# Decoding float64 weights: the rebiased bits in a PSUM buffer of the transposes, the three low bits from ScalarE

## The chip, the cores and the metric

The kernel runs on one core of a Trainium2 chip. The metric is the device time of one execution in microseconds (us). The core's engines each work through their own queue in order: TensorE (PE in the profile, its weight loads as PEld), VectorE (DVE), ScalarE (ACT), GpSimd (POOL); SyncE (SP) issues the loads. All but GpSimd reach PSUM, the memory that TensorE writes, which has eight banks of 128 x 512 fp32; all reach SBUF.

## The reference

Sliding-window attention with a linear position bias (8 batches, 8 heads, 576 positions, 64 per head), then a feed-forward block over its 4608 x 512 output. q, k and v arrive as float32, the weights `w_in` and `w_out` as float64, and the output is float32.

```
scores = q @ k.T / 8 - slope[h] * |i - j|        where 0 <= i - j < 128, else -1e9
attn   = softmax(scores)
x      = (attn @ v), heads side by side           # 4608 x 512
h      = x @ w_in                                 # w_in 512 x 2048
out    = (h * sigmoid(1.702 * h)) @ w_out         # w_out 2048 x 512
```

## The kernel before

The host hands over the weights as the raw 64-bit words of their float64 values, cut into 16 blocks of `w_in` and 16 of `w_out` (each 128 x 512 words). `fetch` (line 201) loads a block into SBUF with an SP transfer; `decode` (line 210) makes fp32 of it on the chip and then splits that into a rounded part and the rest, both in TensorE's fp32 format, so that a product can be summed from three matmuls.

A float64 is two 32-bit words. The upper one (`top`) holds the sign, the 11 bits of the exponent and the first 20 of the mantissa; the lower one (`low`) holds the rest, of which an fp32 needs the three uppermost. The steps of one block, by line:

- L218, ScalarE: `top`, read as an fp32, times 2 to the power of -112. This takes the difference of the two exponents' offsets off, and goes to `c`, a tile of 128 x 512 of the SBUF pool's tag "o" (three buffers, shared with `xb` of L410 and L411).
- L219, VectorE: `low` shifted right by 29, in place; its three uppermost bits are left.
- L220, VectorE: `c` shifted left by 3, or-ed with `low`.
- L221, VectorE: the sign bit of `top` or-ed into `c`. Now `c` is the fp32.
- L224, ScalarE: `c` rounded into the first half of `res`. L225, GpSimd: `c` less that, into the second half.

Attention runs in units of one to three blocks of rows. A function `tick` (line 510) does one step of a pipeline over the units: scores on TensorE (`s_ps`, L303 and L309), the bias and the row minimum on VectorE (L321), the exponent on ScalarE (L332), the division by the row sum (L340, L341, then L345 on GpSimd for the first 24 units, L347 on ScalarE or L349 on VectorE for others), the transposes on TensorE (`flip`, L364) into a PSUM tile `t_ps` of which there are two buffers, their way out (L375 on ScalarE, and for all but the first 24 units the rest on VectorE, L381), and the product with v (L393, L398). PSUM is full: two banks for `acc`, two for `h_ps`, one for `s_ps`, one for `x_ps`, two for `t_ps`.

The feed-forward block works on chunks of 256 rows (`Job`): for each of 16 blocks f, `up` (12 matmuls, L452, then L457 on ScalarE, L458 on VectorE, L461 on ScalarE, L462 on GpSimd) and `down` (6 matmuls, L471). `split_x` (L436, L438) prepares a chunk.

The main loop (from line 585) goes through the pairs of job and block in order. Ahead of each it decodes as many blocks as the weights' due times ask for (`owed`, line 588), and does as many ticks as the due times of attention's outputs ask for (`pace`). Blocks 0 of both weights are decoded in the loop before it. The first chunk uses only the first 8 blocks at first and gets the others after the second chunk, so that the last weights are due later. So the 32 decodings lie in the first part of the program, beside the attention of the first two batches and the first steps of the feed-forward block.

The kernel writes no waits: the framework (Tile) derives them from the tiles. It also sets the order of the instructions on each engine, by a simulated timeline made when the program is built (`schedule_with_timeline_sim=True`), in which an instruction that opens a tile waits until one of its tag's buffers is free. Only the SP transfers keep the program's order (`move`).

Of the kernel before, what the change touches and what calls it, by code (L numbers as in the profile page):

```python
# [8 lines left out]
F32 = mybir.dt.float32  # L9
F32R = mybir.dt.float32r  # L10
BF16 = mybir.dt.bfloat16
I32 = mybir.dt.int32
I64 = mybir.dt.int64
AF = mybir.ActivationFunctionType
ALU = mybir.AluOpType
PSUM = bass.MemoryType.PSUM
# [4 lines left out]
P = 128  # L21
# [135 lines left out]
def tile_kernel(ctx: ExitStack, tc: tile.TileContext, qT, kT, v, w_in, w_out, out):  # L157
    nc = tc.nc
# [5 lines left out]
    ffn = ctx.enter_context(tc.tile_pool(name="ffn", bufs=2))  # L164
    ps = ctx.enter_context(tc.tile_pool(name="ps", bufs=1, space=PSUM))

    def move(dst, src):

        tc.keep_in_program_order(nc.sync.dma_start(dst, src))
# [4 lines left out]
    bias = [const.tile([P, 2 * P], BF16, name=f"bias{h}") for h in range(H)]  # L174
# [26 lines left out]
    def fetch(src, name):  # L201
        st = const.tile([P, 512], I64, name="r" + name, tag=name)
        move(st, src)
        return st
# [5 lines left out]
    def decode(st, name):  # L210

        words = st.bitcast(I32).rearrange("p (m two) -> p m two", two=2)
        top, low = words[..., 1], words[..., 0]
        c = ffn.tile([P, 512], I32, name="wc", tag="o", bufs=3)

        nc.scalar.activation(c.bitcast(F32), top.bitcast(F32), AF.Copy, scale=2.0 ** -112)  # L218
        nc.vector.tensor_scalar(low, low, 29, None, ALU.logical_shift_right)  # L219
        nc.vector.scalar_tensor_tensor(c, c, 3, low, ALU.logical_shift_left, ALU.bitwise_or)  # L220
        nc.vector.scalar_tensor_tensor(c, top, -0x80000000, c, ALU.bitwise_and, ALU.bitwise_or)  # L221
        w = c.bitcast(F32)
        res = const.tile([P, 2, 512], F32R, name=name, tag=name)
        nc.scalar.copy(res[:, 0], w)  # L224
        nc.gpsimd.tensor_tensor(res[:, 1], w, res[:, 0].bitcast(F32), ALU.subtract)  # L225
        return res
# [101 lines left out]
    def exponents(u):  # L328
        u.sums = att.tile([P, 2], F32, name="sums", bufs=3)
        for e, b in enumerate(u.blocks):  # L330
            live = b.p[:b.rows, b.live:b.end]
            nc.scalar.activation(  # L332
                live, live, AF.Exp, bias=u.mins[:b.rows, e:e + 1], scale=-1.0,
                accum_out=u.sums[:b.rows, e:e + 1],
            )

    def normal(u, on_act):
# [4 lines left out]
        for e, b in enumerate(u.blocks):  # L342
# [3 lines left out]
            elif on_act:  # L346
                nc.scalar.activation(live, live, AF.Copy, scale=u.rec[:rows, e:e + 1])  # L347
            else:
# [92 lines left out]
    class Job:  # L441
# [6 lines left out]
        def up(self, f):  # L448
# [7 lines left out]
            g = ffn.tile([P, T], F32, name="g")  # L456
            nc.scalar.activation(g, h, AF.Tanh, scale=0.851)  # L457
            nc.vector.scalar_tensor_tensor(g, g, 1.0, h, ALU.add, ALU.mult)  # L458
# [97 lines left out]
    while ticks < due[0][0] + 3:  # L556
        tick()
        spin(SPINS)
        fetch_upto(ticks - FETCH_TICK)
        if ticks == DECODE_TICK:  # L560
            w1[0] = decode(w1[0], f"w1_0")
        if ticks == DECODE_TICK + 1:
            w2[0] = decode(w2[0], f"w2_0")
# [21 lines left out]
    for now, (j, f) in enumerate(flat):  # L585

        if halves < 2 * NF:
            owed += max(
                (2 * g + 2 - halves - owed) / max(need[g] - DECODE_AHEAD - now, 1)
                for g in range(halves // 2, NF))  # L590
            while owed >= 1 and halves < 2 * NF:
                owed -= 1
                g, ws = halves // 2, (w1, w2)[halves % 2]
                fetch_upto(g + 1 + FETCH_AHEAD)
                ws[g] = decode(ws[g], f"w{1 + halves % 2}_{g}")
                halves += 1
# [64 lines left out]
```

## Time and profile before

| | |
|---|---|
| time, median of 3 runs | 1099.26 us (1097.17 to 1099.34) |
| span of the profiled execution, first to last instruction | 1094.0 us |
| its own time | not recorded; the median is 5.3 us above the span |
| mean granted TensorE clock | 0.990 |

The profile's page first gives the busy time of each engine, then the span in 40 slices of 27 us with the busy share in tenths, then DMA, the chain of work that ended last, and the costliest groups of instructions: line, engine, operation, tiles written and read, shape, count, busy time, mean duration, and the idle time of the engine just before them with the instruction that ended it. A busy TensorE isn't one at its peak, since the ends of pipelined matmuls are modelled. Idle time of an engine that is not the bound costs nothing.

### The profile page before, as it was taken

How to read it: one execution, taken by the hardware profiler on the slowest of the kernel's cores; microseconds unless marked ns; L12 is line 12 of the kernel's file. 1: busy time of each engine (PE TensorE's matmuls, PEld its weight loads, DVE VectorE, ACT ScalarE, POOL GpSimd, SP SyncE). 2: the span in 40 equal slices, each digit the busy share in tenths (PEclk: the TensorE clock that was granted, in tenths of full speed). 3: DMA queues.
4: the chain of work that ended last, by engine and by line, in shares of the span. 5: the costliest groups of instructions: out<-in, count | busy, mean ns of one | idle time of the engine just before them, and what ended most of it. 6: DMA issues, size and time to landing. Idle time of an engine off the chain costs nothing.

```text
span 1094.0 us, 21796 instructions
## 1 busy us (share of the span) xinstructions
PE 1059.8 (97%) x7021; PEld 944.6 (86%) x7021; DVE 745.2 (68%) x2331; ACT 592.2 (54%) x1765; POOL 658.9 (60%) x931
## 2 busy tenths in 40 slices
PE   8888889999999999999999999999999999999998
PEld 5565668999998999999999998999999999998997
DVE  4999798778898687754575768676877677423131
ACT  4665565566675665543555556655565556322222
POOL 4998877567677666644565666665666666323232
PEclk9999889999999999999999999999999999999999
DMA  5965213232242222201222222221222212000000
GB/s 142 332 171 160 69 46 86 72 82 74 84 105 86 65 84 65 84 23 48 54 67 53 84 55 84 65 84 51 73 76 65 76 46 78 1 20 20 1 20 19
DMA packets 97265, 81.24 MB, mean 74 GB/s; under 512 B 50048, under 2 KB 88448, under 8 KB 97152
## 3 DMA queue, kind: packets, MB, share of 16 engines
q1 hardware_dynamic: 91968, 70.42, 23.4%
q10 hardware_dynamic: 5184, 9.44, 2.3%
q8 instruction: 55, 0.90, 0.4%
q14 instruction: 58, 0.48, 0.1%
HBM read 70.39 MB, written 9.44 MB: 73 GB/s over the span
## 4 chain that ended last, share of the span: by engine, by line
PE 82%; DVE 3%; issue 1%; POOL 0%; ACT 0%; DVEq 0%; POOLq 0%
PE h_ps L452 34%; PE acc L471 34%; PE x_ps L398 5%; PE s_ps L309 5%; PE t_ps L364 4%; DVE pb L349 0%; DVE xh L436 0%; DVE pb L321 0%; DVE K L294 0%; DVE rec L340 0%; DVE xf L429 0%; DVE wc L221 0%; DVE g L458 0%; DVE pl L381 0%; DVE o L487 0%
## 5 line engine op out<-in xcount | busy, mean ns | idle before, releaser
L452 PE MATMUL h_ps<-xh,w 128*128 128x256 f32 x2304 | 370.5, 285 | 8.8 <-DVE g L458 4.2
L462 POOL TENSOR_TENSOR gl<-g,gh 128x256 fp32r<-128x256 f32 x288 | 218.6, 759 | 262.2 <-ACT gh L461 198.2
L452 PEld LDWEIGHTS h_ps<-xh,w 128*128 128x128 f32 x2304 | 329.5, 189 | 41.2 <-DVE g L458 6.6
L471 PE MATMUL acc<-w,gh 128*128 128x512 f32 x1152 | 326.8, 401 | 1.1 <-DVE xf L479 1.1
L458 DVE SCALAR_TENSOR_TENSOR g<-g,h_ps 128x256 f32<-128x256 f32 x288 | 119.4, 415 | 181.3 <-ACT g L457 179.6
L457 ACT ACTIVATE g<-h_ps 128x256 f32<-128x256 f32 x288 | 109.8, 382 | 209.7 <-PE h_ps L452 192.4
L471 PEld LDWEIGHTS acc<-w,gh 128*128 128x128 f32 x1152 | 197.6, 189 | 28.7 <-issue 1.3
L452 PE MATMUL h_ps<-xl,w 128*128 128x256 f32 x1152 | 195.9, 281 | 0.0
L461 ACT CAST gh<-g 128x256 fp32r<-128x256 f32 x288 | 116.7, 405 | 145.9 <-DVE g L458 136.4
L471 PE MATMUL acc<-w,gl 128*128 128x512 f32 x576 | 189.0, 403 | 0.0
L332 ACT ACTIVATE pb<-pb,mins 128x256 f32<-128x256 f32 (+3 forms) x292 | 141.2, 484 | 64.9 <-DVE mins L321 61.7
L296 POOL TENSOR_TENSOR K<-rk,K 128x384 fp32r<-128x384 f32 (+1 forms) x140 | 127.3, 909 | 80.7 <-ACT Q L276 24.9
L452 PEld LDWEIGHTS h_ps<-xl,w 128*128 128x128 f32 x1152 | 164.2, 189 | 5.8 <-DVE xl L438 0.3
L321 DVE CUSTOM_DVE_ANT_0 pb<-s_ps,bias 128x256 f32<-128x256 f32 (+5 forms) x320 | 114.2, 376 | 14.7 <-PE s_ps L309 6.5
L349 DVE TENSOR_SCALAR pb<-pb,rec 128x256 f32<-128x256 f32 (+2 forms) x252 | 110.1, 473 | 3.5
L295 POOL TENSOR_TENSOR Q<-rq,Q 64x256 fp32r<-64x256 f32 (+1 forms) x140 | 98.0, 700 | 21.6 <-ACT Q L276 4.4
L364 PE MATMUL t_ps<-ident,pb 128*128 128x128 f32 (+1 forms) x548 | 100.8, 275 | 8.2 <-DVE pb L349 6.6
L471 PEld LDWEIGHTS acc<-w,gl 128*128 128x128 f32 x576 | 93.0, 190 | 8.0 <-issue 0.5
L340 DVE TENSOR_SCALAR rec<-sums 128x2 f32<-128x2 f32 (+2 forms) x164 | 55.1, 336 | 59.6 <-ACT pb L332 58.4
L309 PE MATMUL s_ps<-K,Q 128*128 128x256 f32 (+1 forms) x504 | 91.9, 290 | 2.6 <-POOL gl L462 1.4
L381 DVE TENSOR_TENSOR pl<-t_ps,ph 128x512 fp32r<-128x512 f32 (+2 forms) x140 | 84.0, 602 | 5.2 <-ACT ph L375 4.8
L294 DVE CAST K<-rk 128x384 fp32r<-128x384 f32 (+1 forms) x140 | 59.0, 422 | 41.0 <-PE s_ps L309 31.6
(56 smaller groups left out, 1305.7 us busy)
## 6 DMA issues: line engine op xcount, KB each, us to landing
rk<-kT SPq DMA_DIRECT2D x84, 192.0 KB, 2.7
rq<-qT SPq DMA_DIRECT2D x112, 128.0 KB, 2.6
out<-o ACTq DMA_DIRECT2D x36, 256.0 KB, 2.1
rw<-w_in SPq DMA_DIRECT2D x16, 512.0 KB, 5.9
rw<-w_out SPq DMA_DIRECT2D x16, 512.0 KB, 7.0
rk<-kT SPq DMA_DIRECT2D x56, 128.0 KB, 2.3
rv<-v SPq DMA_DIRECT2D x100, 64.0 KB, 2.0
rq<-qT SPq DMA_DIRECT2D x44, 64.0 KB, 2.4
```

What stands on the lines that cost most here:

```text
L296: nc.gpsimd.tensor_tensor(K2, rk, K1.bitcast(F32), ALU.subtract)
L309: nc.tensor.matmul(u.s[:b.rows, e, b.first:b.end], u.Q[:, b.q0 - u.q0:b.q0 - u.q0 + b.rows], k[:, ko:ko + b.end - b.first], start=(z == 0) ...
L321: nc.vector.tensor_tensor_reduce(b.p[ra:rb, cs:b.end], u.s[ra:rb, e, cs:b.end], bias[head][ra:rb, cs:b.end], -SCALE, BIG, ALU.add, ALU.min ...
L332: nc.scalar.activation(live, live, AF.Exp, bias=u.mins[:b.rows, e:e + 1], scale=-1.0, accum_out=u.sums[:b.rows, e:e + 1],)
L349: nc.vector.tensor_scalar(live, live, u.rec[:rows, e:e + 1], None, ALU.mult)
L364: nc.tensor.transpose(u.t[:c.n, w:w + b.rows], b.p[:b.rows, col:col + c.n], ident[:b.rows, :b.rows])
L452: nc.tensor.matmul(h, w1[f][:, z, k * P:(k + 1) * P], x[:, k], start=(n == 0), stop=(n == len(ops) - 1))
L457: nc.scalar.activation(g, h, AF.Tanh, scale=0.851)
L458: nc.vector.scalar_tensor_tensor(g, g, 1.0, h, ALU.add, ALU.mult)
L461: nc.scalar.copy(gh, g)
L462: nc.gpsimd.tensor_tensor(gl, g, gh.bitcast(F32), ALU.subtract)
L471: nc.tensor.matmul(acc, g[:, t * P:(t + 1) * P], w2[f][:, z], start=(f == self.f0 and n == 0), stop=(f == self.f1 - 1 and n == 2))
```

## The change

The rebiased bits (`c` before) get a PSUM tile of the transposes' tag `t_ps`, one of the same two buffers, and the fp32 result a tile of tag "o" of its own, from L221 on. The three low bits come from ScalarE instead of VectorE's shift: a copy reads `part`, the upper 16 bits of `low`, as an integer, multiplies it by 2 to the power of -13, subtracts not quite a half, and rounds to an integer, which is that word's upper three bits; it writes it over `low`. L220 and L221 do the same operations as before, L220 in place in PSUM, L221 from PSUM and SBUF into SBUF. L224 and L225 are the same.

```diff
+U16 = mybir.dt.uint16
...
         words = st.bitcast(I32).rearrange("p (m two) -> p m two", two=2)
         top, low = words[..., 1], words[..., 0]
-        c = ffn.tile([P, 512], I32, name="wc", tag="o", bufs=3)
-        nc.scalar.activation(c.bitcast(F32), top.bitcast(F32), AF.Copy, scale=2.0 ** -112)
-        nc.vector.tensor_scalar(low, low, 29, None, ALU.logical_shift_right)
-        nc.vector.scalar_tensor_tensor(c, c, 3, low, ALU.logical_shift_left, ALU.bitwise_or)
-        nc.vector.scalar_tensor_tensor(c, top, -0x80000000, c, ALU.bitwise_and, ALU.bitwise_or)
-        w = c.bitcast(F32)
+        part = st.bitcast(U16).rearrange("p (m four) -> p m four", four=4)[..., 1]
+        bits = ps.tile([P, 4 * P], F32, name="w_ps", tag="t_ps", bufs=2).bitcast(I32)
+        w = ffn.tile([P, 512], F32, name="wc", tag="o", bufs=3)
+        nc.scalar.activation(bits.bitcast(F32), top.bitcast(F32), AF.Copy, scale=2.0 ** -112)
+        nc.scalar.activation(low, part, AF.Copy, bias=2.0 ** -14 - 0.5, scale=2.0 ** -13)
+        nc.vector.scalar_tensor_tensor(bits, bits, 3, low, ALU.logical_shift_left, ALU.bitwise_or)
+        nc.vector.scalar_tensor_tensor(w.bitcast(I32), top, -0x80000000, bits, ALU.bitwise_and, ALU.bitwise_or)
         res = const.tile([P, 2, 512], F32R, name=name, tag=name)
         nc.scalar.copy(res[:, 0], w)
         nc.gpsimd.tensor_tensor(res[:, 1], w, res[:, 0].bitcast(F32), ALU.subtract)
```

## The prediction

> **What bounds the kernel now.** I read the page first: its totals, then its slices of the span.
>
> ```profile
> span 1094.0 us, 21796 instructions
> PE 1059.8 (97%) x7021; PEld 944.6 (86%) x7021; DVE 745.2 (68%) x2331; ACT 592.2 (54%) x1765; POOL 658.9 (60%) x931
> PE   8888889999999999999999999999999999999998
> DVE  4999798778898687754575768676877677423131
> ```
>
> Over the whole span TensorE (PE) is the bound: 34.2 us of 1094.0 are idle, so no change to another engine can win more than that plus what a slower clock cost. The slices say where the 34 us are: PE stands at 8 in the first six slices (and the last one), and in four of these six VectorE (DVE) stands at 9. The decoding of the weights lies there, as its first and last lines show (the view of one line's instructions: ns least/median/greatest, then the first and the last start in us):
>
> ```profile
> L219 DVE TENSOR_SCALAR rw<-rw x32: 399/426/2573, 22.0 to 103.7; 128x512 int32<-128x512 int32 x32
> L225 POOL TENSOR_TENSOR w<-wc,w x32: 1260/1339/1787, 27.0 to 165.1; 128x512 fp32r<-128x512 f32 x32
> ```
>
> It begins at 22.0 us and ends 1.3 us after 165.1. I cut the span there with the windows view.
>
> ```profile
> core 0: us, PE busy (x) PEld busy (x) DVE busy (x) ACT busy (x) POOL busy (x), PEclk, DMA share, GB/s
> 22.00:166.00 144.00, 118.86 (x655) 88.58 (x654) 132.65 (x326) 88.66 (x241) 122.69 (x115) 0.93 0.53 159
> 166.00:1094.00 928.00, 921.96 (x6269) 843.94 (x6267) 603.24 (x1958) 494.75 (x1498) 525.83 (x797) 1.00 0.22 60
> ```
>
> The second stretch is PE alone (6.0 us idle in 928). The first is not: PE is idle 144.00 - 118.86 = 25.1 us, DVE is busy 132.65 of 144 (92%), GpSimd (POOL) 122.69 (85%), ScalarE (ACT) 88.66 (62%). The granted clock is 0.93. The view of waits, for PE in this stretch, tells whom PE idles for (columns: total us, times, longest):
>
> ```profile
> PE t_ps L364 <- DVE pb L349: 6.0, 5, 2.0
> PE h_ps L452 <- DVE g L458: 3.7, 5, 1.3
> PE h_ps L452 <- ACT w L224: 2.5, 2, 2.1
> PE s_ps L303 <- DVE mins L321: 2.2, 2, 1.7
> PE h_ps L452 <- DVE xh L436: 2.0, 3, 1.1
> PE s_ps L309 <- POOL gl L462: 1.4, 1, 1.4
> PE s_ps L309 <- DVE mins L321: 1.2, 1, 1.2
> PE acc L471 <- DVE xf L479: 1.1, 1, 1.1
> ```
>
> The six DVE rows are 6.0 + 3.7 + 2.2 + 2.0 + 1.2 + 1.1 = 16.2 us of the 25.1; none of them is a decoding instruction. They are attention and feed-forward work that stood in DVE's queue behind the decoding. ACT has 2.5 and POOL 1.4. So in this stretch a late DVE is what ends most of PE's waits, and the change takes load off DVE.
>
> **The change part by part.** Everything is per half of a weight block; there are 32 of them, all in this stretch. The groups of instructions by line, for DVE between 22 and 166 us (busy us, mean ns | idle before):
>
> ```profile
> L220 DVE SCALAR_TENSOR_TENSOR wc<-wc,rw 128x512 int32<-128x512 int32 x32 | 29.0, 907 | 1.0 <-ACT wc L218 0.6
> L221 DVE SCALAR_TENSOR_TENSOR wc<-rw,wc 128x512 int32<-128x512 int32 x32 | 25.7, 803 | 0.1
> L219 DVE TENSOR_SCALAR rw<-rw 128x512 int32<-128x512 int32 x32 | 22.7, 709 | 1.6 <-DMA rw<-w_out 1.1 <-DMA rw<-w_in 0.5
> L381 DVE TENSOR_TENSOR pl<-t_ps,ph 128x512 fp32r<-128x512 f32 x2 | 1.4, 678 | 0.0
> ```
>
> *The shift (L219) goes:* 32 x 0.709 = 22.7 us of DVE. *L220 and L221 stay* but read one operand from PSUM instead of two from SBUF. The nearest row is L381, same size, one PSUM and one SBUF input, 678 ns. At 0.68 us each they save 29.0 - 21.8 = 7.2 and 25.7 - 21.8 = 3.9 us. No row shows DVE writing PSUM. Upwards the gain ends at 12.1 us (L220 and L221 at their fastest, 662 and 671, below); downwards there may be a loss: if reading and writing the same bank doubled L220's 662 ns, it would cost 13.4 us more, and DVE would lose only 22.7 + 3.9 - 13.4 = 13.2 us (then PE gains some 10% of its waits on DVE, 1.6 us). I take 11.1, because L381 is the nearest row. Why a PSUM input should help shows in the instructions of each line, beside L219's above:
>
> ```profile
> L220 DVE SCALAR_TENSOR_TENSOR wc<-wc,rw x32: 662/775/1680, 23.1 to 161.8; 128x512 int32<-128x512 int32 x32
> L221 DVE SCALAR_TENSOR_TENSOR wc<-rw,wc x32: 671/684/1415, 25.6 to 163.5; 128x512 int32<-128x512 int32 x32
> L381 DVE TENSOR_TENSOR pl<-t_ps,ph x140: 397/676/694, 131.2 to 940.9; 128x512 fp32r<-128x512 f32 x80, 128x384 fp32r<-128x384 f32 x36, 128x256 fp32r<-128x256 f32 x24
> ```
>
> The three decoding lines have a floor (399, 662, 671) and a tail of two to six times it; L381 has no tail at all, 694 at most. The worst shift, in the timeline (start, us):
>
> ```profile
> 103.33 0.76 POOL L345 TENSOR_SCALAR pb<-pb,rec 64x192 f32<-64x192 f32 x1 [1.49 <-DVE rec L340]
> 103.74 2.57 DVE L219 TENSOR_SCALAR rw<-rw 128x512 int32<-128x512 int32 x1
> 104.06 1.28 POOL L225 TENSOR_TENSOR w<-wc,w 128x512 fp32r<-128x512 f32 x1
> 105.30 0.72 POOL L462 TENSOR_TENSOR gl<-g,gh 128x256 fp32r<-128x256 f32 x1
> ```
>
> It covers three POOL instructions and ends 0.3 us after the last of them: a 0.40 us operation that sat behind POOL. In sum DVE loses 22.7 + 11.1 = 33.8 of 132.65 us: 98.9 are left, 69% of today's stretch.
>
> *ScalarE takes a second pass.* Its groups in the stretch:
>
> ```profile
> L218 ACT ACTIVATE wc<-rw 128x512 f32<-128x512 f32 x32 | 21.4, 672 | 3.0 <-DMA rw<-w_out 1.7 <-DVE xf L429 1.3
> L224 ACT CAST w<-wc 128x512 fp32r<-128x512 f32 x32 | 19.9, 620 | 17.0 <-DVE wc L221 11.0 <-DVE rec L341 5.4
> L375 ACT COPY pw<-t_ps 128x512 f32<-128x512 f32 x8 | 4.6, 581 | 2.0 <-PE t_ps L364 2.0
> ```
>
> The new pass reads one of four 16-bit words and writes every second 32-bit word. L218 (every second word in, dense out) takes 672, dense L224 620: stepping one side costs 52 ns, so both sides give about 672 + 52 = 724 at most and 620 at least. I take 0.67, the row with one stepped side: 32 x 0.67 = 21.4 us. ACT goes from 88.66 to 110.1 us, 76% of 144. L218 itself now writes PSUM; no row shows such a write, and I leave it at 672 (the 52 ns either way are 1.7 us of ACT, off PE's path). What that load costs PE I scale from the one ACT wait shown, 2.5 us: 110.1 / 88.66 would make it 3.1; I take +1, from nothing to +3 if it doubles.
>
> The Trainium skill (ScalarE: Activation LUTs, Rules for kernel authors) says the opposite of this edit: plain multiplications and additions go to VectorE, not ScalarE. Rows agree for the bare operation: 399 ns on DVE against some 670 on ACT, so by the rule 32 x 0.27 = 8.6 us of engine time are lost. But the mean shift took 709, so as this kernel runs ACT is not slower.
>
> *POOL's work is the same*, but waits of its own may shorten:
>
> ```profile
> L225 POOL TENSOR_TENSOR w<-wc,w 128x512 fp32r<-128x512 f32 x32 | 45.6, 1434 | 5.7 <-ACT w L224 4.6 <-DVE pb L349 1.1
> ```
>
> At its least (1260 ns, above) L225 would be 40.3, so at most 5.3 us of 122.69; I count nothing.
>
> *DMA:* no transfer is added or moved; the raw tile is read and overwritten as before, the low words now by ACT. The buffer of tag "o" is taken at L221 in place of L218, so it is free more of the time; I count nothing.
>
> *The added wait.* The rebiased bits no longer have a place among three SBUF buffers but take one of the two t_ps buffers of the transposes. So L218 may wait for a flip to be read out, with exponents, copies out of PSUM and tanh behind it on ACT, and all of PE behind those; and a transpose may wait on PE for L221 of a decoding, with everything of PE behind it. How full two buffers would be: in the stretch there are 26 flips (21 from the first row, 8 + 5 + 8 whole ones, and 5 from the second) and 32 decodings.
>
> ```profile
> L375 ACT COPY pw<-t_ps x29: 204/213/588, 21.6 to 122.4; 128x512 f32<-128x512 f32 x8, 128x64 f32<-128x64 f32 x8, 64x64 f32<-64x64 f32 x8, 128x384 f32<-128x384 f32 x5
> L375 ACT CAST ph<-t_ps x5: 457/479/587, 128.8 to 162.2; 128x384 fp32r<-128x384 f32 x3, 128x512 fp32r<-128x512 f32 x2
> ```
>
> How long a decoding holds its buffer, in the timeline (start, us):
>
> ```profile
> 25.15 0.70 ACT L218 ACTIVATE wc<-rw 128x512 f32<-128x512 f32 x1 [1.31 <-DMA rw<-w_out]
> 29.28 0.67 DVE L221 SCALAR_TENSOR_TENSOR wc<-rw,wc 128x512 int32<-128x512 int32 x1
> 88.59 0.68 ACT L218 ACTIVATE wc<-rw 128x512 f32<-128x512 f32 x1
> 94.53 0.69 DVE L221 SCALAR_TENSOR_TENSOR wc<-rw,wc 128x512 int32<-128x512 int32 x1
> ```
>
> These two hold their bits 4.8 and 6.6 us from L218's start to L221's end, 5.7 on average. The bare work is 0.67 + 0.67 + 0.68 + 0.68 = 2.7. A flip holds its buffer 1.2 us at least (four transposes in 0.6, the copy 0.58). With bare work the two buffers are held 32 x 2.7 + 26 x 1.2 = 118 of 288 us, 41%; with today's holding 214 of 288, 74%. Both are held at once for 0.41 x 0.41 = 17% of the flips (4.4 of them, half a hold of 1.35 each: 6 us) or for 55% (14 of them, 2.85 each: 40 us). PE has other work to be put ahead of a late flip; a third of the wait landing on PE is my choice: +2 us with bare work, +13 with today's holding. DVE's queue gets shorter, so I take 2 and keep 13 as the bound.
>
> *What PE gains.* Of the 16.2 us, at least the share of DVE's load that goes (33.8 / 132.65 = 25%): 4.1. At most all. A row of the same kernel in which DVE is busy 81%:
>
> ```profile
> 170.00:400.00 230.00, 228.21 (x1579) 208.83 (x1578) 186.70 (x621) 145.32 (x450) 153.26 (x234) 1.00 0.29 79
> ```
>
> There PE idles 1.8 us in 230, so well below 92% DVE stops ending PE's waits; but the first 25 us of the stretch have little feed-forward work to fill holes. I take 10, the middle of 4.1 and 16.2. Sum: -10 + 1 + 2 = **-7 us**. The span would be 1087.0; what lies around it is taken as the median less the span, 1099.26 - 1094.0 = 5.3, since the profiled execution's own time is not given: **1092.3 us**. The granted clock might rise from 0.93, each 0.01 being 1.3 us of 118.86; I count nothing and keep -4 as its bound.
>
> **The rivals.** *All of it comes.* DVE's 16.2 us go whole, POOL runs free of the decoding's DVE work, the buffers cost nothing: 1099.3 - 16.2 = 1083. For it: L381 without a tail, the row at 81%. Against: POOL at 85% is next. The Trainium skill (SBUF — State Buffer, Who interferes with whom) has the rule: a DVE instruction in a two-port mode, or with two SBUF inputs, and a GpSimd one lock each other out for their whole length, and one SBUF input frees both. By it all 96 decoding instructions on DVE leave the lock; the trace agrees with 2573 against 399 ns.
>
> *ACT becomes the late one.* 76% busy with in-order copies, exponents and tanh; each of the DVE waits above is preceded or followed by an ACT step, and 10 us saved come back as ACT waits: 1099, no change. Against: ACT's own waits on PE's list are only 2.5 now.
>
> *The two buffers bind* (the other side). ACT starts decodings early, as now, DVE takes 5.7 us, transposes wait: -10 + 1 + 13 = +4, 1103.3, and 1106 if DVE gains only the middle of 4.1 and 10. It decides from 9 us of PE waiting on t_ps, 0.35 us for each of the 26 flips. For it: up to three decodings overlap today, since wc has three buffers. Against: the program's order is made with the two buffers known, so other work of PE can stand ahead of a transpose that has to wait.
>
> **How the numbers follow.** Forecast 0.48 (own range 1088 to 1096.5), all of it 0.14, ACT late 0.13, buffers bind 0.25. About 0.2% (2.2 us) is what a measurement of this kernel can tell from no change. Faster: 0.48 + 0.14, less 0.02 of the forecast's upper edge: 0.60. Same: 0.13 + 0.02: 0.15. Slower: 0.25. The range reaches from 1082 (all of it, with a little clock) to 1105.
>
> **What would show it.** Right: DVE near 99 us in the stretch, L220 and L221 at 0.68 without tails, PE's idle time before the last L225 near 18 us, its DVE rows near 6, few waits of L364 or of ACT for a DVE wc. Wrong: PE rows "t_ps L364 <- DVE" on the decoding's lines over 9 us; ACT idle before L218; L220 over 0.9 when it writes PSUM; or a stretch after 166 us that idles.

## The result, and the profile after

Measured on one chip, four runs each: 1069.15 us with the change (1067.95 to 1072.22), 1098.51 before (1097.17 to 1099.34), ratio 0.9741 with a 95% interval of 0.9723 to 0.9759. That is 29.4 us less; the prediction had 7, and its range ended at 1082. The sign was right, the size was not. A few executions of these kernels ran far longer at a lower clock (one of 1291.35 us at 0.746); every time and ratio here is of the others.

The page of the changed kernel (totals, then two rows of slices and the granted clock). In its line numbers the decoding is L219 (rebiased bits to PSUM) and L220 (low bits) on ACT, L221 and L222 (the two or-s) on DVE, L224 on ACT and L225 on POOL.

```profile
span 1070.4 us, 21794 instructions
PE 1054.6 (99%) x7021; PEld 941.6 (88%) x7021; DVE 706.7 (66%) x2299; ACT 605.4 (57%) x1797; POOL 636.1 (59%) x931
PE   7999999999999999999999999999999999999998
DVE  4767898879897777654676668767867687413131
PEclk9799999999999999999999999999999999999999
```

PE's row is 9 from the second slice to the last but one. The span is 23.6 us shorter: PE is idle 15.8 us instead of 34.2 (18.4 less) and busy 5.2 us less with the same 7021 matmuls. The clock can be some 3.4 us of that, by an estimate from the mean granted clocks of the two profiles, 0.990 and 0.993 (0.010 of 1094.0 less 0.007 of 1070.4); the rest isn't accounted for. What is left of the 29.4 us, 5.8, lies between the profiled runs and the medians: the profiled run after took 1072.22, the slowest of its four.

Beside each other, the stretch of the decoding and what follows. First before, cut at the end of the last L225 to the tenth (windows view, columns as in the prediction):

```profile
22.00:166.40 144.40, 119.26 (x657) 88.96 (x656) 133.04 (x328) 89.06 (x243) 123.09 (x116) 0.93 0.53 159
166.40:1094.00 927.60, 921.56 (x6265) 843.56 (x6263) 602.84 (x1955) 494.35 (x1496) 525.43 (x796) 1.00 0.22 60
```

Then after, cut in the same way, with three pieces of its start:

```profile
22.00:144.60 122.60, 116.27 (x663) 87.76 (x664) 91.59 (x272) 100.65 (x265) 98.16 (x109) 0.94 0.61 187
144.60:1070.40 925.80, 919.83 (x6262) 842.12 (x6261) 605.90 (x1981) 496.84 (x1507) 527.99 (x803) 1.00 0.21 61
...
22.00:32.00 10.00, 7.70 (x26) 4.50 (x27) 7.02 (x19) 7.53 (x20) 3.98 (x4) 0.61 0.97 290
32.00:42.00 10.00, 9.84 (x39) 6.12 (x37) 3.98 (x19) 5.31 (x17) 5.57 (x8) 0.71 0.88 269
42.00:52.00 10.00, 8.86 (x54) 6.64 (x52) 8.72 (x23) 10.00 (x24) 7.91 (x8) 1.00 1.00 345
```

Read the first two numbers and PE's count: about the same 660 matmuls take 122.6 us where they took 144.4, so 21.8 of the 23.6 us come out of this stretch. The rest of the program is 1.8 us shorter. PE's idle time in the stretch falls from 25.1 to 6.3 us. DVE is busy 91.6 of 122.6 us (75%, before 92%), ACT 82%, POOL 80%. The clock in the first 20 us is 0.61 and 0.71, lower than in the kernel before, which had 1.00 and 0.83 there. Its own low pieces came later, and the two lowest are those in which PE was busy least:

```profile
122.00:132.00 10.00, 6.74 (x30) 5.37 (x30) 9.91 (x22) 5.74 (x16) 8.47 (x10) 0.73 0.30 78
142.00:152.00 10.00, 6.84 (x34) 5.51 (x33) 8.75 (x19) 4.44 (x12) 8.97 (x11) 0.75 0.09 28
```

What PE still waits for in this stretch, from the view of waits; this is the whole list:

```profile
PE x_ps L393 <- ACT pw L375: 2.1, 1, 2.1
PE h_ps L452 <- DVE g L458: 1.6, 1, 1.6
PE h_ps L452 <- POOL w L225: 1.1, 1, 1.1
PE s_ps L303 <- DMA rk<-kT: 0.8, 2, 0.6
PE s_ps L303 <- DVE mins L321: 0.6, 3, 0.3
PE h_ps L452 <- ACT w L224: 0.3, 1, 0.3
```

Of the six DVE rows, 16.2 us together, two are left with 2.2. No row names t_ps: no transpose waited for a decoding's buffer. The whole list of before has two DVE rows more, under one us each:

```profile
PE x_ps L393 <- DVE wc L221: 0.9, 1, 0.9
PE x_ps L393 <- DVE x L427: 0.6, 1, 0.6
```

So DVE's rows fell from 17.7 to 2.2 us, those of all others from 7.2 to 4.3.

The groups of the stretch by line (busy us, mean ns, then idle before):

```profile
L221 DVE SCALAR_TENSOR_TENSOR w_ps<-w_ps,rw 128x512 int32<-128x512 int32 x32 | 22.2, 692 | 7.9 <-ACT w_ps L219 4.8 <-ACT rw L220 2.7
L222 DVE SCALAR_TENSOR_TENSOR wc<-rw,w_ps 128x512 int32<-128x512 int32 x32 | 21.8, 682 | 1.0
L220 ACT ACTIVATE rw<-rw 128x512 int32<-128x512 uint16 x32 | 21.8, 686 | 2.4 <-DMA rw<-w_in 2.0 <-DMA rw<-w_out 0.2
L219 ACT ACTIVATE w_ps<-rw 128x512 f32<-128x512 f32 x32 | 20.4, 636 | 3.1 <-DMA rw<-w_in 3.0
L225 POOL TENSOR_TENSOR w<-wc,w 128x512 fp32r<-128x512 f32 x32 | 42.3, 1326 | 5.4 <-ACT w L224 5.3
L345 POOL TENSOR_SCALAR pb<-pb,rec 128x256 f32<-128x256 f32 x19 | 17.5, 931 | 7.7 <-DVE rec L341 4.7 <-ACT w_ps L219 2.3 <-ACT w L224 0.8
```

The row to set beside the last one, from the same view of the kernel before:

```profile
L345 POOL TENSOR_SCALAR pb<-pb,rec 128x256 f32<-128x256 f32 x19 | 27.2, 1442 | 1.7 <-DVE rec L341 1.7
```

The decoding's part of DVE is 22.2 + 21.8 = 44.0 us, where the prediction's three rows gave 77.4: 33.4 less. But POOL, whose instructions the change doesn't touch, has shortened as well. L345 took 1442 ns and takes 931 (9.7 us), L225 took 1434 and takes 1326 (3.3 us). Over the whole span POOL's 931 instructions are busy 636.1 us, where they were 658.9.

The view of one line's instructions (least/median/greatest):

```profile
L221 DVE SCALAR_TENSOR_TENSOR w_ps<-w_ps,rw x32: 669/696/705, 24.6 to 140.6; 128x512 int32<-128x512 int32 x32
L222 DVE SCALAR_TENSOR_TENSOR wc<-rw,w_ps x32: 669/684/691, 25.5 to 141.8; 128x512 int32<-128x512 int32 x32
L219 ACT ACTIVATE w_ps<-rw x32: 609/632/674, 23.4 to 139.5; 128x512 f32<-128x512 f32 x32
```

The greatest of the two DVE lines are 705 and 691 ns, where they were 1680 and 1415. The tails are gone.

### The profile page after: what moved, and what is told of

Its sections match the earlier page's. It is cut to its first block, busy times and chain, and to the rows that moved or that the text cites. A ratio compares the mean times of both kernels' runs of the same rounds, so it can differ in the third digit from the quotient of the medians.

```text
span 1070.4 us, 21794 instructions
## 1 busy us (share of the span) xinstructions
PE 1054.6 (99%) x7021; PEld 941.6 (88%) x7021; DVE 706.7 (66%) x2299; ACT 605.4 (57%) x1797; POOL 636.1 (59%) x931
## 4 chain that ended last, share of the span: by engine, by line
PE 93%; DVE 3%; ACT 2%; DMA 1%; issue 1%; POOL 0%; SPq 0%; DVEq 0%; POOLq 0%; ACTq 0%
PE h_ps L452 37%; PE acc L471 37%; PE x_ps L398 5%; PE t_ps L364 5%; PE s_ps L309 5%; PE s_ps L303 1%; PE x_ps L393 1%; PE acc L197 1%; DMA rk<-kT 1%; DMA rw<-w_in 1%; DVE pb L321 1%; ACT pb L332 0%; ACT rw L220 0%; DVE xh L436 0%; SPq L170 0%
## 5 line engine op out<-in xcount | busy, mean ns | idle before, releaser
L462 POOL TENSOR_TENSOR gl<-g,gh 128x256 fp32r<-128x256 f32 x288 | 215.7, 750 | 255.8 <-ACT gh L461 194.4
L321 DVE CUSTOM_DVE_ANT_0 pb<-s_ps,bias 128x256 f32<-128x256 f32 (+5 forms) x320 | 114.6, 377 | 25.3 <-PE s_ps L303 15.5
L340 DVE TENSOR_SCALAR rec<-sums 128x2 f32<-128x2 f32 (+2 forms) x164 | 51.1, 312 | 61.3 <-ACT pb L332 60.0
L381 DVE TENSOR_TENSOR pl<-t_ps,ph 128x512 fp32r<-128x512 f32 (+2 forms) x140 | 84.1, 603 | 5.4 <-ACT ph L375 5.1
L294 DVE CAST K<-rk 128x384 fp32r<-128x384 f32 (+1 forms) x140 | 57.5, 411 | 34.2 <-PE s_ps L309 30.2
```

What stands on the lines that cost most here:

```text
L321: nc.vector.tensor_tensor_reduce(b.p[ra:rb, cs:b.end], u.s[ra:rb, e, cs:b.end], bias[head][ra:rb, cs:b.end], -SCALE, BIG, ALU.add, ALU.min ...
L462: nc.gpsimd.tensor_tensor(gl, g, gh.bitcast(F32), ALU.subtract)
```

## The experiments

There are three questions: what part of the change brings the time, whether the engines' loads or their waiting for each other decide it, and how far one planned order of instructions sways the result. Each ratio is against runs of the kernel before on the same chip; "the stretch" is 22 us to the end of the last subtraction (L225), so its length differs from run to run; the kernel before has 25.1 us of PE idle there and the changed one 6.3.

### Half of the change at a time

Only the low bits from ScalarE, everything else as before (against the kernel before; the lines that define `part` are those of the change):

```diff
-        nc.vector.tensor_scalar(low, low, 29, None, ALU.logical_shift_right)
+        nc.scalar.activation(low, part, AF.Copy, bias=2.0 ** -14 - 0.5, scale=2.0 ** -13)
```

> Only the shift is moved to ScalarE; the rebiased bits stay in their SBUF tile. VectorE loses 22.7 us of decoding, but L220 and L221 still read two SBUF tiles. Theory 'load' (TensorE waits in proportion to VectorE's own busy time; 22.7 of the 33.4 us that the full change takes off): two thirds of the gain of 29 us, 1079 us. Theory 'turns' (VectorE and GpSimd hold each other up whenever VectorE's instruction is one of the tailed kind; 32 of 96 such instructions are gone): one third, 1089 us, and L220 and L221 keep means near 0.9 and 0.8 us. Theory 'plan' (the new order of instructions is what helps): no relation, anything from 1069 to 1100.

Measured: 1088.16 us, ratio 0.9926 (0.9905 to 0.9947). Its page's totals, the stretch, and the two or-s (here L222 and L223):

```profile
PE 1061.5 (97%) x7021; PEld 945.9 (87%) x7021; DVE 736.9 (68%) x2299; ACT 606.6 (56%) x1797; POOL 656.1 (60%) x931
```

```profile
22.00:160.20 138.20, 120.14 (x652) 90.10 (x652) 122.09 (x290) 103.75 (x273) 118.59 (x112) 0.90 0.55 166
```

```profile
L223 DVE SCALAR_TENSOR_TENSOR wc<-rw,wc 128x512 int32<-128x512 int32 x32 | 32.6, 1018 | 0.4
L222 DVE SCALAR_TENSOR_TENSOR wc<-wc,rw 128x512 int32<-128x512 int32 x32 | 29.4, 920 | 4.3 <-ACT wc L220 2.5 <-ACT rw L221 1.8
```

Instructions of 22.7 us are gone from DVE, but DVE's busy time over the span fell only by 8.3 (745.2 to 736.9). The or-s, unchanged, went from 907 and 803 to 920 and 1018 ns: part of the shift's tail is now the neighbours'. A tail is waiting, and it isn't removed with the instruction that showed it. The time is the one that 'turns' gave, but its durations held for the first or only: the second, put near 0.8 us, took 1.02.

Only the bits in PSUM, the shift still on VectorE (against the changed kernel):

```diff
-        nc.scalar.activation(low, part, AF.Copy, bias=2.0 ** -14 - 0.5, scale=2.0 ** -13)
+        nc.vector.tensor_scalar(low, low, 29, None, ALU.logical_shift_right)
```

> Only the bits move to a transposes' PSUM buffer; the shift stays on VectorE. Load: VectorE loses 7.2 + 3.9 = 11 us of 33.4, one third of the gain, 1089 us. Turns: 64 of 96 tailed instructions lose their tail, two thirds, 1079 us; GpSimd's L345 gets shorter by 8 of the 12.6 us. Buffers bind: with decodings holding a buffer longer than the 3.1 us of the full change, TensorE rows 't_ps L364 <- DVE' on decoding lines appear, and the time is above 1089.

Measured: 1088.69 us, 0.9917 (0.9887 to 0.9947); PE idle 15.0 us of the stretch. Its totals, and one row of PE's waits:

```profile
PE 1059.7 (97%) x7021; PEld 944.1 (87%) x7021; DVE 729.6 (67%) x2331; ACT 593.0 (55%) x1765; POOL 641.7 (59%) x931
```

```profile
PE t_ps L364 <- DVE wc L222: 2.9, 2, 1.6
```

DVE is 15.6 us less busy and POOL 17.2, with the same count of instructions on both. The shift, the one decoding instruction still without a PSUM operand, takes 677 ns on average in this run (least 410, greatest 2137). The time is the one that 'load' gave (1089), and 'turns' (1079) missed, although the 40 instructions of L345 did shorten by 10.3 us (45.7 to 35.4). So each theory is right about one half of the change and wrong about the other. The row on t_ps is the wait that the rival of the two buffers named. It is there when DVE is late, at 2.9 us, far from the 9 at which that rival would decide.

To have the price of ScalarE's second pass by itself: the kernel before with the shift left out and nothing in its place. L220 combines with a column of zeros, and the three low bits are left out (the lines that make the column aren't shown).

```diff
-        nc.vector.tensor_scalar(low, low, 29, None, ALU.logical_shift_right)
-        nc.vector.scalar_tensor_tensor(c, c, 3, low, ALU.logical_shift_left, ALU.bitwise_or)
+        nc.vector.scalar_tensor_tensor(c, c, 3, zeros, ALU.logical_shift_left, ALU.bitwise_or)
```

> The kernel before without the shift (the three low bits are left out; L220 combines with a column of zeros, spread over the row): 22.7 us less on VectorE, nothing added on ScalarE. 'VectorE's load decides': 1078 us. 'Turns': L221 gets longer as in the run that moved the shift to ScalarE (1.02 us), and the time is near that run's 1089 to 1092, 1084 to 1090. What this run and that one differ by is the price of ScalarE's second pass there, 0 to 8 us.

Measured: 1090.82 us, 0.9932 (0.9917 to 0.9948), just above what 'turns' gave. The low bits from ScalarE gave 0.9926: the pass cost nothing that can be measured in the kernel before.

### Do VectorE and GpSimd hold each other up?

The kernel before, with VectorE's work untouched and GpSimd's L225 replaced by a fill with zeros. The rests of the weights are left out.

```diff
-        nc.gpsimd.tensor_tensor(res[:, 1], w, res[:, 0].bitcast(F32), ALU.subtract)
+        nc.gpsimd.memset(res[:, 1].bitcast(F32), 0.0)
```

> The kernel before with GpSimd's subtraction L225 replaced by a memset of the same tile (the rests of the weights are left out): some 27 us less on GpSimd, the same on VectorE but with less of GpSimd to wait for. 'VectorE's load decides': VectorE stays the busiest, 1090 to 1098 us. 'Both at once': with GpSimd out of the way VectorE's tailed instructions get shorter (L219 near 0.55, L220 near 0.8 us), 1080 to 1088 us.

Measured: 1081.74 us, 0.9843 (0.982 to 0.9865). Totals, the stretch, and the groups of the decoding's lines:

```profile
PE 1058.5 (98%) x7021; PEld 945.6 (88%) x7021; DVE 720.6 (67%) x2331; ACT 592.5 (55%) x1765; POOL 629.5 (58%) x931
```

```profile
22.00:153.40 131.40, 119.39 (x655) 91.05 (x653) 105.84 (x300) 84.93 (x226) 89.42 (x108) 0.90 0.57 170
```

```profile
L220 DVE SCALAR_TENSOR_TENSOR wc<-wc,rw 128x512 int32<-128x512 int32 x32 | 23.2, 728 | 2.1 <-ACT wc L218 2.0
L221 DVE SCALAR_TENSOR_TENSOR wc<-rw,wc 128x512 int32<-128x512 int32 x32 | 22.5, 709 | 0.1
L219 DVE TENSOR_SCALAR rw<-rw 128x512 int32<-128x512 int32 x32 | 17.7, 552 | 2.9 <-DMA rw<-w_in 2.9
L225 POOL MEMSET w<- 128x512 f32 x32 | 17.8, 563 | 14.8 <-ACT pb L332 6.1 <-DVE wc L221 5.5 <-issue 1.3
```

This is the clearest row of the study. DVE has the same 2331 instructions, and is busy 720.6 us instead of 745.2: 24.6 us of its "busy" time were waiting for POOL. The decoding's three lines alone go from 77.4 to 63.4 us, and PE's idle time in the stretch from 25.1 to 12.0, although the rows that name POOL among PE's waits before are only 2.3 us. So the time before was set by DVE and POOL together, and relief on either side helps both.

The same fill in the changed kernel, the rests again left out:

> The full change with GpSimd's subtraction L225 replaced by a memset of the same tile (the rests of the weights are left out): some 25 us less on GpSimd. If GpSimd still bounds the stretch: 1055 to 1063 us. If, with VectorE's decoding no longer held up by it, it is one of several at 80%: 1064 to 1072.

Measured: 1069.53 us, 0.9735 (0.9711 to 0.9758), beside 0.9741 for the change. The stretch:

```profile
22.00:141.00 119.00, 115.71 (x654) 87.33 (x655) 89.61 (x270) 99.41 (x262) 73.35 (x109) 0.93 0.61 189
```

POOL is 25 us less busy there, DVE only 2.0, and the time is the same. The same edit that was worth 1.6% before is worth nothing after: most of the mutual waiting is gone, and POOL isn't the bound.

### Load put back on one engine of the changed kernel

Each of these issues one instruction more of the decoding, with the result the same, to see whose time counts now. On VectorE, the second or (L222) twice:

```diff
         nc.vector.scalar_tensor_tensor(w.bitcast(I32), top, -0x80000000, bits, ALU.bitwise_and, ALU.bitwise_or)
+        nc.vector.scalar_tensor_tensor(w.bitcast(I32), top, -0x80000000, bits, ALU.bitwise_and, ALU.bitwise_or)
```

> The full change, with the last VectorE instruction of a decoding (one PSUM and one SBUF input, 0.68 us, no tail) done twice: 32 x 0.68 = 21.8 us of VectorE work are back, without a tailed instruction. Load: two thirds of the gain are lost again, 1088 us. Turns: hardly any is lost, VectorE goes from 75% to about 90% of its stretch with GpSimd undisturbed: 1074 us, L345 on GpSimd stays at 0.93 us.

On VectorE, an instruction without a PSUM operand (a shift by nothing) behind ScalarE's low bits:

```diff
         nc.scalar.activation(low, part, AF.Copy, bias=2.0 ** -14 - 0.5, scale=2.0 ** -13)
+        nc.vector.tensor_scalar(low, low, 0, None, ALU.logical_shift_right)
```

> The full change, with a shift by zero bits of the low words on VectorE between ScalarE's pass and the combination: the removed instruction (0.40 us bare, SBUF to SBUF, in place) is back, ScalarE's pass stays. Load by bare time: 12.8 us back, 1080 us, less loss than the run with the doubled PSUM instruction. Turns: its mean is again 0.6 to 0.7 us, L345 on GpSimd goes from 0.93 back over 1.1 us, and it loses more than the run with the doubled PSUM instruction although its bare time is smaller: 1080 to 1085 us against 1074.

On ScalarE, L219 twice:

```diff
         nc.scalar.activation(bits.bitcast(F32), top.bitcast(F32), AF.Copy, scale=2.0 ** -112)
+        nc.scalar.activation(bits.bitcast(F32), top.bitcast(F32), AF.Copy, scale=2.0 ** -112)
```

> The full change, with ScalarE's rebias into PSUM done twice: 32 x 0.636 = 20.4 us more on ScalarE, nothing more on VectorE or GpSimd. ScalarE then has 121 us of work for a stretch that now takes 123. 'ACT late' (the rival of the prediction): it becomes the bound and 10 to 20 us are lost, 1079 to 1089 us, with TensorE waiting for ScalarE's copies and casts. 'VectorE alone decides': 1069 to 1073 us. Between them: the loss per us added is smaller than for VectorE (20 us lost for 21.8 added).

On GpSimd, L225 twice for the blocks of `w_in`:

```diff
-        nc.gpsimd.tensor_tensor(res[:, 1], w, res[:, 0].bitcast(F32), ALU.subtract)
+        for _ in range(2 if name.startswith("w1") else 1):
+            nc.gpsimd.tensor_tensor(res[:, 1], w, res[:, 0].bitcast(F32), ALU.subtract)
```

> The full change, with GpSimd's subtraction L225 done twice for the 16 blocks of w_in: 16 x 1.3 = 21 us more on GpSimd, no more on VectorE or ScalarE. GpSimd's busy time fell by 25 us with the change. If GpSimd's relief is part of the gain: 1080 to 1088 us. If only VectorE's load counts: 1069 to 1073 us.

| put back on the changed kernel | us | ratio to before (95%) | PE idle in the stretch |
|---|---|---|---|
| nothing | 1069.15 | 0.9741 (0.9723 to 0.9759) | 6.3 |
| VectorE, PSUM operand | 1089.13 | 0.9918 (0.9888 to 0.9947) | 12.8 |
| VectorE, SBUF only | 1083.67 | 0.9877 (0.985 to 0.9905) | 16.4 |
| ScalarE | 1088.12 | 0.9904 (0.9883 to 0.9925) | 14.9 |
| GpSimd, 16 instructions | 1099.17 | 1.0006 (0.9991 to 1.0021) | 22.9 |

Some 20 us of load on any of the three gives back 14 to 30 us. I had looked for one engine whose load costs and two whose load is free; there is none. For GpSimd the price, 30 us, is above both forecasts, which ended at 1088. For VectorE 'turns' failed: the instruction with a PSUM operand left L345 at 0.93 us, as 'turns' said, and still cost 20.0 us where 'turns' had 5 and 'load' 19; the one without, though its mean was again 671 ns, cost 14.5, not more. So, unless the order made that price, the mutual waiting isn't all: work on VectorE that doesn't lengthen GpSimd's costs nearly its own length too. PE's greatest waits with the load on GpSimd:

```profile
PE h_ps L453 <- DVE g L459: 7.8, 4, 3.3
PE x_ps L394 <- ACT pw L376: 4.9, 7, 2.1
PE h_ps L453 <- POOL w L226: 2.8, 1, 2.8
```

And with the load on ScalarE:

```profile
PE acc L472 <- ACT gh L462: 2.9, 1, 2.9
PE x_ps L394 <- ACT pw L376: 2.6, 2, 2.2
```

The engine that was loaded is named only in part: a load on GpSimd shows as lateness of DVE and ACT. Part of each price may also be another order of all instructions, which the next runs measure.

### The clock at the start, and the order of instructions

The changed kernel without the dummy matmuls, which compute nothing, that the program puts between the first ticks (SPINS):

```diff
-SPINS = 3
+SPINS = 0
```

> The full change without the dummy matmuls that stand between the first ticks (33 of 65 dropped, some 4 us of TensorE work that computes nothing). Theory 'clock' (a hole in TensorE's work lowers the granted clock for some 10 to 20 us after it, so a hole costs about twice): the clock between 22 and 60 us falls below the 0.61 and 0.71 seen, and the time stays or rises, 1069 to 1076 us. Theory 'holes alone': TensorE has less to do, 1066 us.

Measured: 1082.02 us, 0.9845 (0.9827 to 0.9864), above what either theory gave. Windows:

```profile
12.00:22.00 10.00, 9.82 (x27) 5.54 (x28) 3.15 (x17) 3.79 (x14) 4.76 (x7) 0.50 0.37 91
22.00:32.00 10.00, 9.20 (x27) 5.15 (x26) 7.45 (x24) 7.42 (x19) 4.77 (x6) 0.50 1.00 324
32.00:42.00 10.00, 9.86 (x27) 5.51 (x25) 4.52 (x17) 5.32 (x16) 6.31 (x8) 0.50 0.84 270
42.00:52.00 10.00, 10.00 (x32) 6.58 (x31) 4.53 (x17) 4.66 (x13) 2.83 (x4) 0.50 0.98 298
```

PE is busy in all four, at 0.50 of the clock for 40 us, and does 27 matmuls in ten us. Its idle time in the stretch is 6.1 us, as with the change (6.3), and 15.8 us in the whole span, as with the change, and yet the profiled span is 8.0 us longer and the median 13. So that loss is the clock's. What lowers it is argued, not shown: without the dummies PE stands idle for 0.7 us twice between 7.6 and 10.1 us, where the changed kernel has 0.3 each time, and the low clock follows at 12.

In the changed kernel the clock's low piece after 22 us follows a hole at the first decoding. ACT's timeline there (start, busy us; in brackets the idle time and its releaser):

```profile
20.14 0.19 ACT L332 ACTIVATION_READ_ACCUMULATOR pb<-pb,mins 128x1 f32 x1
23.37 0.62 ACT L219 ACTIVATE w_ps<-rw 128x512 f32<-128x512 f32 x1 [3.04 <-DMA rw<-w_in]
23.93 0.64 ACT L220 ACTIVATE rw<-rw 128x512 int32<-128x512 uint16 x1
24.47 0.46 ACT L375 COPY pw<-t_ps 128x384 f32<-128x384 f32 x1
```

ACT stands 3.04 us at L219, whose block hasn't landed; the copy of a transpose queues behind it, and PE's longest wait (2.1 us, for `pw`, to 25.0 us) is for that copy. In pieces of 2 us the clock is 1.00 up to 24 us, 0.50 to 0.55 from 24 to 38 while PE is 93 to 100% busy from 26 to 38, then 1.00 again. The hole is thus paid twice here, once as idle time and again as clock, if the clock fell because of it. I tried to decode one tick later:

```diff
-DECODE_TICK = 5
+DECODE_TICK = 6
```

> The full change, with the first two decodings one tick later (the constant 5 becomes 6). In the changed kernel's profile ScalarE waits 3.0 us for the first weights to land, a copy out of PSUM stands behind it, TensorE idles 2.15 us for that copy, and then the clock is 0.61 and 0.71 for 20 us, 6.8 us of clock. Theory 'clock': without that wait both go, 1063 to 1067 us and a granted clock near 1.000 in every run. Theory 'holes alone': 2 us, 1067. If the next wait takes its place: 1069.

Measured: 1078.48 us, 0.9811 (0.9789 to 0.9832). A miss, and the edit didn't take the hole away: ACT still waits 1.95 us for the block, and PE 2.16 us for the copy, to 26.65 us. Only the low clock after it was shorter (0.69, 0.50 and 0.96 in the pieces of 2 us from 26 to 32). The profiled run's mean clock is 0.997, but the four runs have 0.994 to 0.997, where the change had 0.993 to 1.000. PE is idle 14.4 us in the stretch, with new holes between 112 and 142 us. The longest of them is a transpose that waits for a decoding's buffer, as the rival of the two buffers said:

```profile
PE t_ps L364 <- DVE wc L222: 3.0, 1, 3.0
```

Such a row, of 1.8 to 3.8 us, is in seven runs in all: both of the half with the bits in PSUM, both loads on VectorE, the load on ScalarE, the run without dummies and this one. Why the order came out so isn't settled.

So the scatter that the order alone makes has to be known. The number of dummy matmuls ahead of the first load (FIRST_SPINS, 32 in both kernels) changes no work of the decoding, but the planner lays everything out anew.

```diff
-FIRST_SPINS = 32
+FIRST_SPINS = 28
```

The changed kernel with 28 and with 36, and the kernel before with the same:

> The full change with 28 in place of 32 dummy matmuls at the very start (some 0.4 us of TensorE at a time when it waits for the first loads): no engine's load in the decoding changes, but the order that the planner makes does. If the order by itself is worth little ('load'): 1067 to 1071 us. If the order scatters the time ('plan'): 1075 to 1080, as in the run with the first decodings one tick later, and the change itself is worth less than 29 us.

> The same with 36 dummy matmuls: 'load' 1068 to 1072 us, 'plan' anything between 1069 and 1085.

> The kernel before with 28 dummy matmuls: 'load' 1096 to 1100 us; 'plan' 1085 to 1110, with the same scatter as the changed kernel's.

> The kernel before with 36 dummy matmuls: 'load' 1096 to 1100 us; 'plan' 1085 to 1110.

And each half of the change with 36:

> The run with only the shift moved to ScalarE, with 36 in place of 32 dummy matmuls at the start: another order. 1085 to 1093 us if the halves' small gain is their own; 1075 to 1080 if the first run fell on a bad order.

> The run with only the bits in PSUM, with 36 in place of 32 dummy matmuls at the start: 1084 to 1092 us if the small gain is its own, 1075 to 1080 if the first run fell on a bad order.

| ratio to before | 28 | 32 | 36 |
|---|---|---|---|
| before | 1.0022 (1.0007 to 1.0037) | 1 | 1.0014 (1.0 to 1.0028) |
| low bits on ScalarE | | 0.9926 (0.9905 to 0.9947) | 0.9937 (0.9918 to 0.9957) |
| bits in PSUM | | 0.9917 (0.9887 to 0.9947) | 0.9891 (0.9874 to 0.9908) |
| the change | 0.9847 (0.9818 to 0.9877) | 0.9741 (0.9723 to 0.9759) | 0.9766 (0.9746 to 0.9786) |

In us the change stands at 1080.8, 1069.15 and 1071.33. Four dummy matmuls more or less move it by up to 12 us, and the kernel before by at most 0.22%, 2.4 us. The mean of the change's three ratios is 0.9785, so by these three orders some 6 us of the 29 belong to the order that was measured, and the worst of them still wins 17.

Three of the four times (1071.33, 1099.41 and 1098.56 us) lie in the ranges of 'load', which 'plan' covers too; the changed kernel with 28 lies at the upper end of 'plan' alone. Both halves lie in the ranges given for a small gain of their own.

The last run asked for a better kernel: the change with the subtraction of the `w_out` blocks on VectorE, to take load off GpSimd.

```diff
+        sub = nc.vector if name.startswith("w2") else nc.gpsimd
-        nc.gpsimd.tensor_tensor(res[:, 1], w, res[:, 0].bitcast(F32), ALU.subtract)
+        sub.tensor_tensor(res[:, 1], w, res[:, 0].bitcast(F32), ALU.subtract)
```

> The full change with the subtraction for the 16 blocks of w_out on VectorE instead of GpSimd: 21 us less on GpSimd, 16 x 0.7 = 11 us more on VectorE, all of it with two SBUF inputs. By the losses seen per us given back (GpSimd 1.2 to 1.4, VectorE 0.7 to 0.9): a gain of some 10 us at most, 1060 to 1070 us; if VectorE is held up again, 1072 to 1080.

Measured: 1071.21 us, 0.9744 (0.972 to 0.9768), PE idle 5.7 us. It lies between its two ranges and is no better than the change.

## Why the prediction fell short, point by point

- **PE is the bound, and the gain lies in the stretch of the decoding.** Right: 21.8 of the 23.6 us of span come from there.
- **DVE loses 33.8 us.** Right: its decoding lines lose 33.4, and the two or-s take 692 and 682 ns where 680 was taken. The nearest row, L381, served as a price even where the result goes to PSUM (L221); the loss bounded there didn't occur.
- **ACT's second pass, 0.67 us each, PE +1.** The duration was right (686 ns). Its price on PE was nothing by the comparison with the shift left out, in the kernel before; in the changed one, where 20 us more on ACT cost 19, it isn't measured. L219 into PSUM takes 636 ns, 36 less than L218 into SBUF. The Trainium skill (ScalarE: Activation LUTs, Rules for kernel authors) gives plain multiplications and additions to VectorE; the runs differ here, where the mean shift on VectorE took 709 ns.
- **The buffers, PE +2.** Nothing in the end: no wait for t_ps. A decoding holds its buffer 3.1 us on average from L219's start to L222's end, near the 2.7 of bare work, since DVE comes at once. The rival had its mechanism right: with a later DVE a t_ps row of 2.9 us appears, far below its point of 9, and at most 3.8 in any run.
- **"I count nothing" for POOL.** Wrong. Two lines of POOL alone gave 13.0 us of busy time in the stretch, and all of POOL 22.8 over the span. I had bounded L225 by its least duration, at 5.3, and didn't look at L345, whose mean of 1442 ns beside 931 held nearly twice as much.
- **"I take 10, the middle of 4.1 and 16.2".** This is the step that failed. PE's idle time in the stretch fell by 18.8 us (25.1 to 6.3), more than even the upper end, and the +1 and +2 set against the 10 didn't come. Nothing spoke for 10 but its place in the middle. DVE's rows, 17.7 us in the whole list of waits, lost 15.5 of it, nearly all, as the row at 81% suggested; the other rows gave some 3. The lower end, 4.1, let PE's waits shrink in proportion to DVE's busy time; that fell by 31% in the stretch, and PE's waits on DVE by 88%. The runs showed in its place that DVE and POOL held each other up: with POOL's subtraction replaced by a fill and DVE untouched, 24.6 us of DVE's busy time and 13.1 of PE's idle time went. How much of the 18.8 is this waiting, and how much the plain load taken off DVE, isn't separated.
- **"I count nothing" for the clock.** Wrong: PE is busy 5.2 us less with the same matmuls, some 3.4 of them clock by the estimate above. The mean clock was 0.982 to 0.992 in the runs before; after, it was 0.993 in the run of 1072.22 us, 0.995 in that of 1070.21 and 1.000 in those of 1068.1 and 1067.95. The Trainium skill (TensorE: Matmul & The Clock Gate, Part 1: The HAM clock gate) sets the clock by how busy PE has lately been, to half or full, and gives about 3.4 us of work as the way back to full. The half and the full clock agree with the run without dummy matmuls; the way back does not, since there PE stood at 0.50 for 40 us while 92 to 100% busy by the profile, and the kernel was 13 us slower at the same idle time.
- **What lies around the span, 5.3 us.** In the profiled run after it is 1.8 (1072.22 less 1070.4), and 1.7 to 3.4 in all others. So the profiled run of before lay near 1095.8, about 2.7 below the median (an estimate from that 1.8), and the sum should have stood against it.
- **The rivals.** "All of it comes" (1083) was nearest, and had POOL running free in its mechanism, but stopped at the six DVE rows. Its rule in the Trainium skill (SBUF — State Buffer, Who interferes with whom) agrees with the trace: with one PSUM operand the greatest or-s fell from 1680 and 1415 to 705 and 691 ns, while the shift that stayed in SBUF took 677 on average and 2137 at most. The Trainium skill frees an instruction with one SBUF input only outside the two-port modes (same section), a condition that the prediction's last words on the rule left out. The shift has one SBUF input, and no run shows its mode. "ACT becomes the late one" didn't occur, but ACT is no longer far off: 20 us more on it cost 19. "The two buffers bind" didn't occur with the change, and stayed small in the other runs.

What the halves show: taking one of three instructions out of the jam brought 0.6 to 0.7%, relieving the other two 0.8 to 1.1%, and all three 1.5 to 2.6%, depending on the order. The ratios' means (0.69%, 0.96%, 2.15%) would mean that the whole is more than its parts, since a jam with one instruction left still has its tail (677 ns). But the difference, 0.5%, is no larger than what the order alone makes (up to 1.1%), so it isn't settled. Nor is how much of each put-back load's price was load, and how much order.

## What to carry to other kernels

When two engines' instructions have long tails at the same place (here 399 to 2573 ns for one line), their busy times contain waiting for each other: look at the least durations on both sides when pricing a relief, and count the partner engine's time as part of the jam. A kernel whose order is planned from a timeline should be measured in two or three neighbouring orders before a gain is put down to an edit. After such a jam is gone, the engines may be so balanced that 20 us on any of them costs 14 to 30 us, while taking 25 off one of them wins nothing.

## What the runs showed of the hardware

- An or of 128 x 512 on DVE with one operand in PSUM, written in place to PSUM, took 669 to 705 ns, 692 on average; the one that wrote SBUF took 669 to 691, 682 on average.
- ACT wrote 128 x 512 fp32 to PSUM in 636 ns and to SBUF in 672, both from every second word; reading every fourth 16-bit word and writing every second 32-bit word took 686.
- GpSimd's 19 divisions of 128 x 256 took 1442 ns on average beside VectorE's SBUF-only decoding and 931 beside that with PSUM, with nothing changed on them.
- With GpSimd's 32 subtractions replaced by fills, VectorE's same 2331 instructions were busy 720.6 us in place of 745.2.
- The granted clock stayed at 0.50 for 40 us while PE was 92 to 100% busy, where the dummy matmuls at the start were missing. After a wait of PE of 2.15 us it was low for 14 us in the changed kernel, and after one of 2.16 us for some 4 us in the run that decoded one tick later.
